# Fifteen small GpSimd operations of each setup of an S4D kernel, done by VectorE

## The chip, the cores and the metric

The kernel runs on one core of a Trainium2 chip. The metric is the device time of one execution in microseconds; a time is given as the median of several runs. The core has five engines, each with its own queue of instructions that it works off in order: TensorE (PE in the profile, its weight loads PEld), VectorE (DVE), ScalarE (ACT), GpSimd (POOL) and SyncE (SP), which here issues almost all DMA transfers.

## The reference

Four layers follow each other on an input x of 2048 tokens by 512 features, all in float32: an S4D convolution, a routed feed-forward layer, and both once more with the same weights. Each adds its result to x. Cut to what matters:

```
def A(u):                                   # S4D convolution, per feature d
    dt = exp(log_dt)
    A  = -exp(log_A_real) + 1j * A_imag     # 512 x 128
    C  = (C_real + 1j * C_imag) * dt[:, None]
    P  = exp((A * dt[:, None])[:, :, None] * arange(2048))
    K  = 2 * einsum("dn,dnl->dl", C, P).real
    y  = irfft(rfft(u, 4096) * rfft(K, 4096))[:2048]
    return y + u * D_skip

def B(x):                                   # two tokens of 2048, SwiGLU, 512 -> 1792 -> 512
    ...

x = x + A(layernorm(x)); x = x + B(layernorm(x))
x = x + A(layernorm(x)); x = x + B(layernorm(x))
```

The change lies in the preparation of the kernel K: from C_real, C_imag, A_imag, log_A_real and dt, the phase and the magnitude of C and of the powers of exp(A dt) are worked out per state n and feature d.

## The kernel before, in words

The 512 features are worked in four chunks of 128. The first convolution has two halves that run side by side. The first makes K: states lie on the 128 partitions, and for each group of 16 features (class KStep, 32 steps) a phase table and a decay table are built from a few powers, turned into sine and cosine, multiplied, and contracted over the states on TensorE. The second is the convolution itself by a transform in stages, mostly matmuls.

Before the first KStep, `setup` (line 543) turns the parameters into the starting powers. It is called twice: for chunk 0 (tiles of 128 by 128, called small here, in one tile named su) with its results left in SBUF, and for chunks 1 to 3 together (128 by 384, called wide, in tiles named su_w, su_w3b and su_bigB), whose results go to DRAM (pid, prd) and are loaded back per half chunk (tiles near and far). Each call returns a list of single instructions: absolute values of C, the arc tangent of their ratio (L586 to L594), its sine and cosine for the magnitude of C (L596 to L600), the phase by quadrant (L602 to L612), and integer phases of the powers (L615 to L636) and their decays (L641).

What the first setup makes is needed at once: L636 gives the integers from which ScalarE's L500 starts the table "eight" of the first eight phases; GpSimd's L504 and L507 fill that and the table "far", L669 builds a step's phase table, L683 and L688 its decay table. VectorE's L710, L712 and L717 multiply these with ScalarE's sine and cosine (L699, L702) into the tile sc, which TensorE contracts at L725; ScalarE's L729 and VectorE's L732 take the result (kt), TensorE transforms it at L745, and ScalarE's L755 copies that. The tables of a step have two buffers each, sine and cosine one.

In between, the statistics of the input x are taken on VectorE (L1005, 16 instructions over four loads of 1 MB, L1002). The four loads use two buffers in turn, those that later hold the tiles xc and z. So the second load into either waits for the statistics of the first, and the loads of xc and z for the convolution (L441, issued one behind the other on SyncE's queue) wait for the last statistics. Tables made from the statistics (L1013 to L1024) and tile z are what ScalarE's L838 needs, the layer norm in front of the convolution.

The order of everything is written out by hand. `PLAN` gives each unit of work a number, by lane: `setup` and `setup2` are the lists of the two calls, `stat0` the statistics, `table` their tables, `phase8`, `decay8`, `phase`, `decay`, `trig`, `prod_b`, `prod_p` and `contract` the KSteps. All units are sorted by that number and issued in turn, and `in_order` (line 389) ties the instructions of each engine to that order, SyncE's too. An instruction that waits therefore holds everything behind it on its engine. In this order the first setup's units have the numbers 17 to 234, those of VectorE and of the changed operations 22 to 96, mixed with the first of the second setup, with statistics and loads; the second setup's go from 19 to 355. The unit of the first setup's L636 has number 91, that of the wide L598 159, that of the last statistics 161.

Of the kernel before, what the change touches and what calls it, by code (L numbers as in the profile page):

```python
# [14 lines left out]
OP = mybir.AluOpType  # L15
# [29 lines left out]
    w=[52],  # L45
# [357 lines left out]
def build(tc, x, xr, lar, aim, cr, ci, ldt, dsk, wr, wg, wu, wd, d1_h, d1k_h, d4_h, w2_h, w3_h, w3b_h, sm_h, out):  # L403
# [3 lines left out]
    V, A, G, T = nc.vector, nc.scalar, nc.gpsimd, nc.tensor  # L407
    AX = mybir.AxisListType.X
    ctx = ExitStack()
    with ctx, in_order(tc, ORDER):  # L410
# [132 lines left out]
        def setup(c0, c1, room, direct=False):  # L543
# [6 lines left out]
            crt, cit, im, lr, sw, mx = (at_(i) for i in range(6))  # L550
            pc, ip = pair(26), pair(28).bitcast(I32)
            ar, ai, w, at, al = (at_(i) for i in range(20, 25))
# [24 lines left out]
            S = []  # L577
# [9 lines left out]
            S.append(lambda: A.activation(ai, cit, AF.Abs))  # L587
            S.append(lambda: V.tensor_tensor(mx, ar, ai, op=OP.max))
            S.append(lambda: V.tensor_tensor(sw, ar, ai, op=OP.min))
            S.append(lambda: G.tensor_scalar(w, mx, 1e-37, None, op0=OP.max))  # L590
            S.append(lambda: V.reciprocal(w, w))
            S.append(lambda: G.tensor_tensor(w, sw, w, op=OP.mult))
            S.append(lambda: A.activation(at, w, AF.Arctan))
            S.append(lambda: V.tensor_tensor(w, ai, ar, op=OP.is_gt))  # L594
            S.append(lambda: A.activation(al, lr, AF.Exp))
            S.append(lambda: A.activation(ar, at, AF.Sin))  # L596
            S.append(lambda: A.activation(ai, at, AF.Sin, scale=-1.0, bias=halfpi))
            S.append(lambda: G.tensor_tensor(mx, mx, ai, op=OP.mult))  # L598
            S.append(lambda: G.tensor_tensor(sw, sw, ar, op=OP.mult))
            S.append(lambda: G.tensor_tensor(mx, mx, sw, op=OP.add))  # L600
            g1, v1 = ar, ai
            S.append(lambda: G.tensor_scalar(g1, at, 1.0 / (2 * math.pi), None, op0=OP.mult))  # L602
            S.append(lambda: G.tensor_scalar(v1, g1, -2.0, 0.25, op0=OP.mult, op1=OP.add))
            S.append(lambda: G.tensor_tensor(v1, v1, w, op=OP.mult))
            S.append(lambda: G.tensor_tensor(g1, g1, v1, op=OP.add))
            S.append(lambda: V.scalar_tensor_tensor(al, al, -1.0, dt, op0=OP.mult, op1=OP.mult))
            S.append(lambda: G.tensor_scalar(v1, g1, -2.0, 0.5, op0=OP.mult, op1=OP.add))
            S.append(lambda: G.tensor_scalar(w, crt, 0.0, None, op0=OP.is_lt))
            S.append(lambda: G.tensor_tensor(v1, v1, w, op=OP.mult))
            S.append(lambda: G.tensor_tensor(g1, g1, v1, op=OP.add))  # L610
            S.append(lambda: G.tensor_scalar(v1, cit, 0.0, -0.5, op0=OP.is_lt, op1=OP.add))
            S.append(lambda: G.tensor_tensor(g1, g1, v1, op=OP.mult))  # L612
            u, gi = im, sw.bitcast(I32)
            bq, bi = pair(8), pair(22).bitcast(I32)
            S.append(lambda: V.scalar_tensor_tensor(u, im, 1.0 / (2 * math.pi), dt, op0=OP.mult, op1=OP.mult))  # L615
# [412 lines left out]

        st1, rd1 = stats_tiles(1)
        late_setup = setup(1, 4, [sb.tile([128, 32, CH], F32, name=f"su1_{k}", tag=k, bufs=1) for k in ("w3", "w3b", "bigB")])  # L1030

        xw = []
# [146 lines left out]
        for f_ in setup(0, 1, [new_big("su0", "A")], True):  # L1179
            put_in("setup", f_)  # L1180
# [686 lines left out]
```

## Time and profile before

| | us |
|---|---|
| median of 3 runs | 535.35 |
| lowest and highest | 533.23, 535.77 |
| the profiled execution, its own time | 532.64 |
| span of the profiled execution | 530.9 |

| engine | busy us | share of the span | instructions |
|---|---|---|---|
| TensorE | 432.4 | 81% | 5428 |
| VectorE | 411.9 | 78% | 957 |
| ScalarE | 385.2 | 73% | 862 |
| GpSimd | 340.0 | 64% | 364 |

The page also draws the span in 40 slices of 13.3 us. TensorE is nearly idle in the first four and nearly full from the eighth on; GpSimd is nearly full from the second to the ninth. The shares are averages over stages with different limits, so the first 140 us are read by stretch, from the views below. A row of a timeline gives the start and the length in us, the engine, the line of the kernel, the operation, what it writes and reads with their shapes, and in brackets how long the engine had been idle before and what ended it. The profiled execution is one of several, so its rows are set against its own time.

### The profile page before, as it was taken

The numbers are of one execution on the slowest core, as the hardware profiler recorded it, in microseconds if no ns is written. First come the engines' busy times: TensorE is split into PE (matmuls) and PEld (weight loads), VectorE is DVE, ScalarE is ACT, GpSimd is POOL, SyncE is SP. The second block draws the span as 40 slices with busy tenths as digits, with TensorE's granted clock in tenths as the row PEclk, the third lists the DMA queues.
The fourth block names the chain that finished last, engine by engine and source line by source line (L and its number), as shares of the span: only waits on it lengthen the run. The fifth ranks groups of instructions, "written<-read, shape, count | busy, mean of one in ns | idle before, by whom it ended". The sixth has DMA issues, their size and how long they took to land. (4 is left out here: it accounts for less than half of the span.)

```text
span 530.9 us, 14080 instructions
## 1 busy us (share of the span) xinstructions
PE 432.4 (81%) x5428; PEld 338.9 (64%) x5428; DVE 411.9 (78%) x957; ACT 385.2 (73%) x862; POOL 340.0 (64%) x364
## 2 busy tenths in 40 slices
PE   1011467999999999999989985899799999998486
PEld 1011345889878987689847853676678888664234
DVE  7878779787888899888977479675567689799851
ACT  6578999999999997889635435451566965769882
POOL 3898999998886778683503942254606878888200
PEclk9999999999999999999999998899799999999779
DMA  6825456988669787967767799536664857752943
GB/s 199 329 86 219 141 199 194 332 224 213 154 171 246 178 201 235 275 174 219 206 193 235 303 343 422 206 120 199 214 224 160 255 140 228 211 200 120 406 188 161
DMA packets 67307, 115.77 MB, mean 218 GB/s; under 512 B 8708, under 2 KB 50984, under 8 KB 62504
## 3 DMA queue, kind: packets, MB, share of 16 engines
q1 hardware_dynamic: 67112, 114.85, 66.8%
q8 instruction: 43, 0.70, 0.6%
q14 instruction: 24, 0.20, 0.1%
q0 software_dynamic: 128, 0.02, 0.0%
HBM read 68.83 MB, written 39.72 MB: 204 GB/s over the span
## 5 line engine op out<-in xcount | busy, mean ns | idle before, releaser
L873 POOL TENSOR_TENSOR y<-p 64x256 f32<-64x256 f32 x76 | 57.6, 758 | 71.0 <-DVE p L858 38.8
L717 DVE TENSOR_TENSOR sc<-tr,mg 128x1024 f32<-128x1024 f32 x64 | 77.0, 1210 | 1.1 <-POOL mg L688 0.8
L725 PE MATMUL pk<-sc 128*32 128x64 f32 x2048 | 39.0, 233 | 46.3 <-DVE sc L717 30.8
L725 PEld LDWEIGHTS pk<-sc 128*32 128x32 f32 x2048 | 33.4, 118 | 58.3 <-ACT tr L699 31.7
L683 POOL TENSOR_TENSOR mg<-eight,far 128x768 f32<-128x768 f32 x32 | 53.6, 1674 | 17.7 <-DVE sc L712 10.0
L669 POOL TENSOR_TENSOR ph<-eight,far 128x768 int32<-128x768 int32 x32 | 53.2, 1665 | 8.7 <-ACT tr L702 8.3
L849 DVE STREAM_TRANSPOSE g<-zf 128x512 f32<-128x512 f32 x64 | 45.5, 712 | 12.9 <-PE zf L845 11.4
L845 PE MATMUL zf<-z,d 128*128 128x256 f32 x192 | 53.6, 411 | 2.2 <-ACT z L1630 1.1
L1102 ACT ACTIVATE w<-pv 128x512 f32<-128x512 f32 x48 | 28.5, 594 | 35.2 <-PE pv L879 19.1
L879 PE MATMUL pv<-y,w 128*128 128x128 f32 x320 | 47.0, 294 | 4.3 <-POOL y L871 4.3
L879 PEld LDWEIGHTS pv<-y,w 128*128 128x128 f32 x320 | 41.8, 201 | 12.3 <-POOL y L871 9.2
L858 DVE TENSOR_TENSOR p<-pu,kf 128x1024 f32<-128x1024 f32 x32 | 38.9, 1219 | 13.1 <-PE pu L768 4.8
L745 PE MATMUL kq<-d1k,kt 128*64 128x128 f32 x512 | 38.5, 297 | 12.6 <-DVE kt L732 11.2
L768 PE MATMUL pu<-g,w 128*64 128x128 f32 x640 | 43.0, 278 | 0.4 <-DVE p L858 0.4
L745 PEld LDWEIGHTS kq<-d1k,kt 128*64 128x64 f32 x512 | 30.2, 147 | 20.7 <-DVE kt L732 15.6
L845 PEld LDWEIGHTS zf<-z,d 128*128 128x128 f32 x192 | 34.6, 198 | 13.5 <-DVE g L849 4.4
L768 PEld LDWEIGHTS pu<-g,w 128*64 128x64 f32 x640 | 36.4, 134 | 7.3 <-issue 4.2
L871 POOL TENSOR_TENSOR y<-p 64x256 f32<-64x256 f32 x52 | 38.4, 739 | 3.0
L688 POOL TENSOR_TENSOR mg<-mg,f32s 128x512 f32<-128x512 f32 x32 | 34.4, 1078 | 8.6 <-ACT mg L677 7.5
L827 PE MATMUL pv<-p,w 128*128 128x128 f32 x192 | 38.7, 283 | 0.0
L827 PE MATMUL pv<-p,w3b 128*128 128x128 f32 x192 | 37.2, 276 | 0.0
L699 ACT ACTIVATE tr<-ph 128x1024 f32<-128x1024 int32 x32 | 32.9, 1028 | 4.7 <-DVE sc L717 3.0
(380 smaller groups left out, 1149.9 us busy)
## 6 DMA issues: line engine op xcount, KB each, us to landing
vd<-w SPq DMA_DIRECT2D x48, 256.0 KB, 2.8
v<-vd SPq DMA_DIRECT2D x24, 512.0 KB, 6.8
kf<-kfd SPq DMA_DIRECT2D x16, 512.0 KB, 4.8
wd<-in_wd SPq DMA_DIRECT2D x4, 2048.0 KB, 12.2
ks<-kd SPq DMA_DIRECT2D x48, 128.0 KB, 3.4
kfd<-kd SPq DMA_DIRECT2D x24, 256.0 KB, 3.8
x<-in_xr SPq DMA_DIRECT2D x4, 1024.0 KB, 6.8
w<-in_w SPq DMA_DIRECT2D x2, 2048.0 KB, 8.1
```

The costliest lines, as they stand in the source:

```text
L669: G.tensor_tensor(self.ph[:, :, 8:32].rearrange("p d (k i) -> p d k i", k=3), self.first(0).rearrange("p d (o i) -> p d o i", o=1).to_broa ...
L683: G.tensor_tensor(mg[:, :, 0:2, 8:32].rearrange("p d t (k i) -> p d t k i", k=3), self.first(1).rearrange("p (d t o) i -> p d t o i", t=2, ...
L717: V.tensor_tensor(sc.rearrange("p d (t i) -> p d t i", t=3)[:, :, 0:3:2, :], t, self.mg[:, :, 0:3:2, :], op=OP.mult)
L725: T.matmul(self.pk[32 * g : 32 * g + 32, e, :], t[:, 0:32], t[:, 32:96], start=k == 1, stop=k == 0, tile_position=(0, 32 * g))
L745: T.matmul(self.pq[64 * ri : 64 * ri + 64, e].rearrange("p k g -> p (k g)"), self.kt[:, e].rearrange("p h b -> p (h b)"), d1k[:, 128 * ri ...
L768: T.matmul(pt[64 * par : 64 * par + 64, ri, q, :], w2[:, k1, 64 * ri : 64 * ri + 64], col(src, k1), start=True, stop=True, tile_position=( ...
L827: T.matmul(pv[:, k, :], w[:, j, :], p[:, t, k % 2, k // 2, :], start=t == 0, stop=t == 1)
L845: T.matmul(pf[:, 16 * s : 16 * s + 16, :], d1[:, 128 * s : 128 * s + 128], z[:, :, 16 * q : 16 * q + 16], start=True, stop=True)
L849: V.transpose(g[:, :, 16 * q : 16 * q + 16, :].rearrange("p k e t -> p e k t"), pf.rearrange("p (k t) e -> p e k t", t=2))
L858: V.tensor_tensor(pp, pu.rearrange("p (o r) q e -> p o r (q e)", o=1).to_broadcast([128, 2, 2, 2 * CH]), kf.rearrange("p r (o q) e -> p r ...
L873: E.tensor_tensor(y[0:64, :, par, :], p[0][ls, 0], p[1][ls, 1], op=OP.subtract)
L879: T.matmul(pv[:, k, :], w3[:, 4 * gi + k, :], y[:, k // 2, k % 2, :], start=True, stop=True)
```

## The change

In `setup`, 15 operations are issued on VectorE (V) instead of GpSimd (G): L590, L592, L598 to L600, L602 to L605 and L607 to L612. Since `setup` is called twice this moves 15 small and 15 wide instructions. What they compute, their operands, their place in PLAN and all else stay as they are.

```diff
--- before.py
+++ after.py
@@ -587,29 +587,29 @@
             S.append(lambda: A.activation(ai, cit, AF.Abs))
             S.append(lambda: V.tensor_tensor(mx, ar, ai, op=OP.max))
             S.append(lambda: V.tensor_tensor(sw, ar, ai, op=OP.min))
-            S.append(lambda: G.tensor_scalar(w, mx, 1e-37, None, op0=OP.max))
+            S.append(lambda: V.tensor_scalar(w, mx, 1e-37, None, op0=OP.max))
             S.append(lambda: V.reciprocal(w, w))
-            S.append(lambda: G.tensor_tensor(w, sw, w, op=OP.mult))
+            S.append(lambda: V.tensor_tensor(w, sw, w, op=OP.mult))
             S.append(lambda: A.activation(at, w, AF.Arctan))
             S.append(lambda: V.tensor_tensor(w, ai, ar, op=OP.is_gt))
             S.append(lambda: A.activation(al, lr, AF.Exp))
             S.append(lambda: A.activation(ar, at, AF.Sin))
             S.append(lambda: A.activation(ai, at, AF.Sin, scale=-1.0, bias=halfpi))
-            S.append(lambda: G.tensor_tensor(mx, mx, ai, op=OP.mult))
-            S.append(lambda: G.tensor_tensor(sw, sw, ar, op=OP.mult))
-            S.append(lambda: G.tensor_tensor(mx, mx, sw, op=OP.add))
+            S.append(lambda: V.tensor_tensor(mx, mx, ai, op=OP.mult))
+            S.append(lambda: V.tensor_tensor(sw, sw, ar, op=OP.mult))
+            S.append(lambda: V.tensor_tensor(mx, mx, sw, op=OP.add))
             g1, v1 = ar, ai
-            S.append(lambda: G.tensor_scalar(g1, at, 1.0 / (2 * math.pi), None, op0=OP.mult))
-            S.append(lambda: G.tensor_scalar(v1, g1, -2.0, 0.25, op0=OP.mult, op1=OP.add))
-            S.append(lambda: G.tensor_tensor(v1, v1, w, op=OP.mult))
-            S.append(lambda: G.tensor_tensor(g1, g1, v1, op=OP.add))
+            S.append(lambda: V.tensor_scalar(g1, at, 1.0 / (2 * math.pi), None, op0=OP.mult))
+            S.append(lambda: V.tensor_scalar(v1, g1, -2.0, 0.25, op0=OP.mult, op1=OP.add))
+            S.append(lambda: V.tensor_tensor(v1, v1, w, op=OP.mult))
+            S.append(lambda: V.tensor_tensor(g1, g1, v1, op=OP.add))
             S.append(lambda: V.scalar_tensor_tensor(al, al, -1.0, dt, op0=OP.mult, op1=OP.mult))
-            S.append(lambda: G.tensor_scalar(v1, g1, -2.0, 0.5, op0=OP.mult, op1=OP.add))
-            S.append(lambda: G.tensor_scalar(w, crt, 0.0, None, op0=OP.is_lt))
-            S.append(lambda: G.tensor_tensor(v1, v1, w, op=OP.mult))
-            S.append(lambda: G.tensor_tensor(g1, g1, v1, op=OP.add))
-            S.append(lambda: G.tensor_scalar(v1, cit, 0.0, -0.5, op0=OP.is_lt, op1=OP.add))
-            S.append(lambda: G.tensor_tensor(g1, g1, v1, op=OP.mult))
+            S.append(lambda: V.tensor_scalar(v1, g1, -2.0, 0.5, op0=OP.mult, op1=OP.add))
+            S.append(lambda: V.tensor_scalar(w, crt, 0.0, None, op0=OP.is_lt))
+            S.append(lambda: V.tensor_tensor(v1, v1, w, op=OP.mult))
+            S.append(lambda: V.tensor_tensor(g1, g1, v1, op=OP.add))
+            S.append(lambda: V.tensor_scalar(v1, cit, 0.0, -0.5, op0=OP.is_lt, op1=OP.add))
+            S.append(lambda: V.tensor_tensor(g1, g1, v1, op=OP.mult))
             u, gi = im, sw.bitcast(I32)
             bq, bi = pair(8), pair(22).bitcast(I32)
             S.append(lambda: V.scalar_tensor_tensor(u, im, 1.0 / (2 * math.pi), dt, op0=OP.mult, op1=OP.mult))
```

## Rows read from the trace of the kernel before

**Rows 1.** Busy time of each engine in four stretches (us from the start of the span; the length; then busy us and instructions of TensorE, its weight loads, VectorE, ScalarE and GpSimd; the granted clock, the busy share of the DMA engines, GB/s).

```profile
21.40:37.26 15.86, 0.00 (x0) 0.00 (x0) 10.87 (x18) 13.01 (x20) 15.38 (x14) 1.00 0.47 174
51.80:77.00 25.20, 11.72 (x240) 9.80 (x240) 18.81 (x22) 24.73 (x47) 24.64 (x23) 1.00 0.52 180
77.00:97.00 20.00, 16.45 (x345) 12.18 (x346) 17.64 (x27) 19.40 (x32) 19.22 (x19) 1.00 0.72 235
97.00:140.00 43.00, 42.62 (x702) 39.34 (x701) 34.58 (x51) 41.47 (x76) 38.92 (x36) 1.00 0.82 227
```

**Rows 2.** The waits of ScalarE from 51 to 97 us: who waited for whom, us in total, times, the longest.

```profile
ACT z L838 <- DVE su_w3b L628: 1.3, 1, 1.3
ACT gk L755 <- PE kq L745: 0.4, 1, 0.4
ACT mg L677 <- POOL eight L504: 0.3, 1, 0.3
```

**Rows 3.** The load of tile z: the last statistics on VectorE, the issue of the load on SyncE's queue, the time to landing in the view of the tile, and the first instruction on ScalarE that reads it (start us, us, engine, line, operation).

```profile
42.25 0.68 DVE L1005 BATCH_NORM_STATS2 stt<-x 128x6 f32<-128x512 f32 x1
...
43.38 0.38 SPq L441 DMA_DIRECT2D z<-in_x  x1
...
DMA to landing us min/median/max: 8.3/8.3/8.3
...
51.79 0.49 ACT L838 ACTIVATE z<-z,bz,rs 128x128 f32<-128x128 f32 x1 [1.27 <-DVE su_w3b L628]
```

**Rows 4.** GpSimd's operations of the setups: busy time and count on the small tile of the first setup from 5 to 20 us, and on the wide tile of the second from 5 to 70 us (all of its operations but L600).

```profile
5.00:20.00 15.00, 7.34 (x15) 1.00 0.83 285
...
5.00:70.00 65.00, 15.56 (x14) 1.00 0.57 205
```

**Rows 5.** VectorE from 7.6 to 21.5 us in order of time (start us, us, operation; in brackets the idle time before it and what ended it).

```profile
7.63 0.67 DVE L588 TENSOR_TENSOR su_w<-su_bigB 128x384 f32<-128x384 f32 x1 [0.28 <-ACT su_bigB L586]
...
8.42 0.88 DVE L615 SCALAR_TENSOR_TENSOR su_w<-su_w,dtb 128x384 f32<-128x384 f32 x1
...
9.95 0.28 DVE L594 TENSOR_TENSOR su<-su 128x128 f32<-128x128 f32 x1
10.15 0.55 DVE L589 TENSOR_TENSOR su_w<-su_bigB 128x384 f32<-128x384 f32 x1
10.62 0.42 DVE L619 TENSOR_TENSOR su<-su 128x256 f32<-128x256 f32 x1
11.07 0.29 DVE L620 TENSOR_SCALAR su<-su 128x256 int32<-128x256 f32 x1
11.28 0.35 DVE L616 TENSOR_SCALAR su_bigB<-su_w 128x384 f32<-128x384 f32 x1
11.55 0.61 DVE L622 TENSOR_SCALAR su_w<-su_w 128x384 f32<-128x384 f32 x1
12.08 0.68 DVE L628 TENSOR_SCALAR far<-su 128x256 int32<-128x256 int32 x2
12.68 0.53 DVE L628 TENSOR_SCALAR su<-su 128x256 int32<-128x256 int32 x1
...
14.16 0.56 DVE L628 TENSOR_SCALAR su<-su 128x256 int32<-128x256 int32 x1
...
18.58 0.96 DVE L625 TENSOR_SCALAR su<-su 128x256 int32<-128x256 f32 x1
19.89 0.23 DVE L634 TENSOR_SCALAR su<-su 128x128 int32<-128x128 f32 x1 [0.34 <-POOL su L600]
20.15 0.29 DVE L635 CUSTOM_DVE_ANT_0 su<-su 128x256 uint16<-128x256 uint16 x1
20.36 0.28 DVE L628 TENSOR_SCALAR su<-su 128x256 int32<-128x256 int32 x1
20.57 0.28 DVE L636 TENSOR_SCALAR su<-su 128x256 int32<-128x256 int32 x1
...
20.97 0.55 DVE L606 SCALAR_TENSOR_TENSOR su_bigB<-su_bigB,dtb 128x384 f32<-128x384 f32 x1
```

**Rows 6.** ScalarE's first sine, its first copy of the first setup's integers, and what that releases on GpSimd.

```profile
11.01 0.31 ACT L596 ACTIVATE su<-su 128x128 f32<-128x128 f32 x1
...
20.89 0.44 ACT L500 ACTIVATE eight<-su 128x256 int16<-128x256 int16 x1 [3.60 <-DVE su L636]
...
21.40 3.58 POOL L504 TENSOR_TENSOR eight<-eight,su 128x128 int32<-128x128 int32 x5 [1.54 <-ACT eight L500]
```

**Rows 7.** VectorE's statistics after the first load that it waits for, GpSimd's second L688, and VectorE's third L717.

```profile
24.69 1.88 DVE L1005 BATCH_NORM_STATS2 stt<-x 128x6 f32<-128x512 f32 x3 [1.97 <-DMA x<-in_xr]
...
36.20 1.06 POOL L688 TENSOR_TENSOR mg<-mg,f32s 128x512 f32<-128x512 f32 x1
...
38.94 1.21 DVE L717 TENSOR_TENSOR sc<-tr,mg 128x1024 f32<-128x1024 f32 x1
```

**Rows 8.** Two wide VectorE operations of one shape in the second setup.

```profile
44.72 0.99 DVE L619 TENSOR_TENSOR su_bigB<-su_bigB 128x768 f32<-128x768 f32 x1
...
64.19 1.79 DVE L624 TENSOR_TENSOR su_w<-su_w,su_bigB 128x768 f32<-128x768 f32 x1
```

**Rows 9.** The waits of ScalarE for L699 from 8 to 52 us.

```profile
ACT tr L699 <- DVE sc L717: 2.6, 1, 2.6
ACT tr L699 <- POOL ph L669: 0.9, 1, 0.9
```

## The prediction

> **What bounds the kernel now.** I read first the table of busy time by stretch [rows 1]. From 97 to 140 us TensorE is busy for 42.6 of 43 us, so whatever comes late or early in the first 97 us is passed on whole by TensorE's fixed order, and nothing of the change lies behind that point. Before 97 us TensorE is half idle and ScalarE and GpSimd are the full engines: from 51.8 to 77 they are busy for 24.73 and 24.64 of 25.2 us. The reader is to see that two engines, not one, are full there. Emptying GpSimd can shorten that stretch only by what ScalarE waits for it. The waits of ScalarE [rows 2] name that: 0.3 us, in one place, beside 0.4 us for TensorE. So I then asked what starts ScalarE's full stretch. It is L838 at 51.79, the first use of tile z; z's load was issued at 43.38 and landed 8.3 us later, at 51.7 [rows 3]. The list of waits puts that stop down to VectorE's L628, but the landing is what fits the time. The load in turn is issued behind the load of xc on SyncE's queue, and xc's buffer is free only after the last statistics, L1005 on VectorE at 42.25 [rows 3]. So the path is: VectorE up to 42.9 us, load of z, ScalarE to about 97 us, TensorE to the end.
>
> **The change, part by part.** GpSimd loses the 15 small operations of the first setup, 7.34 us by the one row that groups them, and the 15 wide ones of the second, of which the row of their tile groups 14 with 15.56 us [rows 4]. On GpSimd this is worth next to nothing by rows 2.
>
> *The first setup on VectorE, to L636.* L636 at 20.57 releases L500 on ScalarE at 20.89, which had waited 3.60 us, and that releases GpSimd's L504 at 21.40 [rows 5, 6]. All 15 small operations now stand ahead of L636 in VectorE's order, and the wide L590 and L592 with them.
> - The first two small ones cost nothing: VectorE waits 0.28 us for ScalarE until 7.63 behind them, and they go in ahead of that without the hand-overs between the two engines [rows 5].
> - The other 13: a small tensor_tensor costs 0.20 from start to start when the next does not need it (L594 at 9.95, L589 at 10.15), and its 0.28 plus 0.03 when it does (L619 takes 0.42 and L620 starts 0.45 after it). A small tensor_scalar costs 0.26 then (L634 to L635) [rows 5]. Half of them feed the next one, so 13 x 0.25 = 3.2 us; 2.6 if none waits, 4.0 if all do.
> - The wide ones: 0.47 for L592 (as the wide L589, 10.15 to 10.62) and 0.3 for L590 (as L616 wide, 11.28 to 11.55) [rows 5]: 0.8 us.
> - A new wait: L599 needs ScalarE's L596, which ends at 11.32 [rows 6]. VectorE gets there at about 10.5 (L619's start at 10.62, 0.3 later for L590, 0.3 to 0.4 earlier for wide L615), because L619 and L620, which ran meanwhile, now stand behind it. 0.8 us, with everything of VectorE queued behind.
> - One wait goes: L634 waited 0.34 for GpSimd's L600 [rows 5].
> - VectorE's other operations get cheaper. Those that ran beside GpSimd's took longer than their twins that did not: wide L615 0.88 against wide L606 0.55; L628 at 12.68 and 14.16 0.53 and 0.56 against 0.28 at 20.36; L625 0.96 against L620's 0.29; wide L622 0.53 from start to start against L616's 0.27; the two L628 at 12.08 0.60 against 0.42 [rows 5]. Given back: 0.33 + 0.25 + 0.28 + 0.67 + 0.26 + 0.18 = 2.0 us.
>
> Sum: 3.2 + 0.8 + 0.8 - 0.3 - 2.0 = 2.5 us later at L636. The bounds are 1.9 (no small operation waits for the one before) and 4.5 (nothing given back). I take 2.5, since each slow row lies beside a GpSimd row and each quick one does not.
>
> The Trainium skill speaks to this on the page SBUF — State Buffer, section Who interferes with whom: a VectorE instruction with two SBUF inputs, or in a two-port mode, and a GpSimd instruction exclude each other, and the second waits until the first is through. The trace agrees in kind (0.88 against 0.55); by the rule the whole 2.0 us comes back, without it none and the sum is 4.5.
>
> *From L636 to the load of z.* VectorE itself has 1.97 us of waiting for a load ahead of L1005 at 24.69 [rows 7]: 0.5 of the 2.5 is left. GpSimd is busy for 15.38 of 15.86 us from 21.40 to 37.26, the end of the second L688 (36.20 + 1.06) [rows 1, 7], so this L688 ends at 39.8, and VectorE's L717, which ran at 38.94, must wait for it: 0.8 us late. The larger counts. Then the wide L598 stands ahead of the last L1005: 0.5 us (0.47 as L589). The load of z goes out 1.3 us late and L838 starts at about 53.1. ScalarE gets there in time: its line, late by about 1.8 through the same L688 and L669, ends 1.27 us ahead of 51.79 today [rows 3]. L599 wide must wait for ScalarE's L596 on VectorE, but the tables that L838 also needs are then ready near 51.6 to 52.5, under the same cover; with the load not late they would decide.
>
> *The second setup, 51.8 to 77 us.* Eight wide operations go into VectorE's order, 0.3 to 0.5 us each by the wide rows [rows 5], some 2.4 to 4.4 us with their waits for each other. VectorE is busy for 18.81 of 25.2 us there [rows 1], so 6.4 us of idle time hide them. GpSimd runs ahead, and the 0.3 us of rows 2 go.
>
> Sum: +1.3 - 0.3 = +1.0 us on the profiled execution's 532.64 (span 530.9). That execution is 2.7 us below the median shown, 535.35. On the median the forecast is 536.3. Its own range: from -0.5 (lower bound, and all of ScalarE's 1.1 us idle time from 51.8 to 97 gone) to +3.4 (L636 late by 4.5, so 2.8 at L717, L598 at 0.88, less 0.3), 534.9 to 538.8.
>
> **The rivals.**
> - *VectorE becomes the bound of 51.8 to 77 us: slower.* GpSimd is still busy there, with L669, L683, L688 and L504, for some 15.7 us (24.64 less eight at 15.56 / 14), and a moved operation with two SBUF inputs may wait for one of them. The price is that of L624, 1.79 us, against 0.99 for L619 of the same shape [rows 8]: 0.8 us more each. Eight operations at 0.5 + 0.8 are 10.4 us, over 6.4 idle, so 4.0 late, with the 1.3 of the load 5.3: 540.6. It decides from a mean of 0.8 us each (6.4 / 8), and is plain to measure from 1.0. For it: VectorE's gaps are few and lie before given instructions. Against: GpSimd is only 60% busy once the moved work is gone, and VectorE's own wide operations gain by that. The Trainium skill has the rule, on SBUF — State Buffer, section Who interferes with whom: the one that starts second blocks fully.
> - *GpSimd was the bound: faster.* If ScalarE's order only follows GpSimd's pace, and the first setup, with no hand-over between two engines, is done sooner, ScalarE's waits go: 2.6 and 0.9 us for L699, 1.3 for L838, 0.3 for L677 [rows 2, 9]. That is 5.1 us: 530.2. For it: GpSimd's full stretch. Against: 2.6 of it hangs on a VectorE instruction and 1.3 on z's load, and neither is GpSimd's.
> - *All of it hidden.* If L636 is late by under 1.9, both waits behind it take it up, and L598's 0.5 less 0.3 is left: 535.5.
>
> **How the numbers follow.** About 0.5%, 2.7 us, can be told from no change. Forecast 0.42 (0.38 of it within that bound, 0.04 slower), VectorE as the bound 0.28 (0.26 slower, 0.02 within), all hidden 0.18 (within), GpSimd as the bound 0.12 (0.10 faster, 0.02 within). So faster 0.10, same 0.60, slower 0.30. The time is that of the likeliest, 536.3. The range takes the forecast's own, nearly all of the hidden case, and the lower two thirds of VectorE's: 533.4 to 540.0.
>
> **What would show it.** In the changed kernel: L636 at 22.5 to 23.5 instead of 20.57; a wait of VectorE for ScalarE's L596 near 10.5; wide L615 near 0.55; GpSimd's L504 at about 23.9; the load of z issued at about 44.7 and L838 at 53.1; ScalarE busy for over 24 of the 25 us behind it, GpSimd for some 15; TensorE full from about 98. The prediction is wrong if L838 keeps its time, if ScalarE's stretch shows gaps that end on VectorE, or if the stretch from L838 to TensorE's full part gets shorter by more than 1 us.

## The result and the profile after

| | before | after |
|---|---|---|
| median of 18 runs, us | 534.85 | 539.95 |
| lowest and highest | 531.95, 538.17 | 535.62, 542.86 |
| the profiled execution, its span | 532.64, 530.9 | 535.62, 533.8 |
| VectorE, GpSimd busy us | 411.9, 340.0 | 422.3, 316.5 |

The ratio is 1.0076, with a 95% interval of 1.0053 to 1.0099: 4.1 us slower (2.8 to 5.3), where 1.0 was forecast; the two medians lie 5.1 us apart. A later comparison of the same two kernels gave 1.0071 (1.0033 to 1.0109). The loss is made before 97 us. As its mark I use VectorE's only L1026, which stands in a fixed place of its order: it starts at 92.71 us before and at 97.34 after, 4.63 later.

```profile
92.71 0.66 DVE L1026 TENSOR_REDUCE swr<-wrt 128x1 f32<-128x512 f32 x1
```

```profile
97.34 0.67 DVE L1026 TENSOR_REDUCE swr<-wrt 128x1 f32<-128x512 f32 x1
```

VectorE in the first setup, after (start us, us, operation, idle time and what ended it), to be read against [rows 5]:

```profile
8.51 0.56 DVE L615 SCALAR_TENSOR_TENSOR su_w<-su_w,dtb 128x384 f32<-128x384 f32 x1
...
11.33 0.29 DVE L599 TENSOR_TENSOR su<-su 128x128 f32<-128x128 f32 x1 [0.72 <-ACT su L596]
...
14.77 0.28 DVE L628 TENSOR_SCALAR su<-su 128x256 int32<-128x256 int32 x1
...
23.25 0.29 DVE L636 TENSOR_SCALAR su<-su 128x256 int32<-128x256 int32 x1
```

The first setup came out as forecast. L636 starts at 23.25 instead of 20.57. VectorE now waits 0.72 us for ScalarE's L596, and wide L615 (0.56) and L628 (0.28) are quick now that GpSimd is silent beside them.

VectorE from there to the load of z, after; [rows 3, 7] answer to it:

```profile
33.73 1.28 DVE L1005 BATCH_NORM_STATS2 stt<-x 128x6 f32<-128x512 f32 x2 [1.56 <-DMA x<-in_xr]
34.93 0.67 DVE L710 SCALAR_TENSOR_TENSOR sc<-tr,mg 128x512 f32<-128x512 f32 x1
...
40.16 1.21 DVE L717 TENSOR_TENSOR sc<-tr,mg 128x1024 f32<-128x1024 f32 x1
...
43.76 0.68 DVE L1005 BATCH_NORM_STATS2 stt<-x 128x6 f32<-128x512 f32 x1
```

Of the 2.7 us, 1.2 are left at L710 (33.70 before). What VectorE waits for ahead of it is a load of x, not GpSimd. The same wait stands there before:

```profile
32.50 1.29 DVE L1005 BATCH_NORM_STATS2 stt<-x 128x6 f32<-128x512 f32 x2 [3.01 <-DMA x<-in_xr]
```

GpSimd's second L688 ends at 39.8 (38.77 + 1.06) as forecast, but VectorE reaches its L717 only at 40.16, straight behind its own work. With L598 and the rest the last statistics start 1.51 us late.

The load of z and the first instruction that uses it, after:

```profile
44.89 0.38 SPq L441 DMA_DIRECT2D z<-in_x  x1
...
DMA to landing us min/median/max: 6.8/6.8/6.8
...
54.90 1.65 ACT L838 ACTIVATE z<-z,bz,rs 128x128 f32<-128x128 f32 x4 [2.51 <-DVE bz L1024]
```

This load takes 6.8 us instead of 8.3: it lands at 51.7 as before, and its late issue costs nothing. With 8.3 us it would have landed at 53.2. L838 starts at 54.90, 3.11 us late, and stops for VectorE's L1024, the end of the tables, through at 54.87. Before, L1024 was through at 50.3, 1.4 us ahead of z. VectorE from the first of the tables to their last, after, and then the same stretch before:

```profile
44.58 0.18 DVE L1015 TENSOR_TENSOR rs<-stt 128x16 f32<-128x16 f32 x1
45.63 0.56 DVE L599 TENSOR_TENSOR su_w<-su_w,su_bigB 128x384 f32<-128x384 f32 x1 [0.87 <-ACT su_bigB L596]
...
46.40 0.90 DVE L600 TENSOR_TENSOR su_w<-su_w 128x384 f32<-128x384 f32 x1
47.22 1.98 DVE L618 CAST su_bigB<-su_bigB 128x768 int32<-128x768 f32 x1
...
49.24 1.69 DVE L619 TENSOR_TENSOR su_bigB<-su_bigB 128x768 f32<-128x768 f32 x1
...
51.98 1.30 DVE L628 TENSOR_SCALAR su_w3b<-su_bigB 128x768 int32<-128x768 int32 x1
...
54.69 0.18 DVE L1024 SCALAR_TENSOR_TENSOR bz<-mv,rs 128x16 f32<-128x16 f32 x1
```

```profile
43.07 0.18 DVE L1015 TENSOR_TENSOR rs<-stt 128x16 f32<-128x16 f32 x1
...
43.49 0.55 DVE L618 CAST su_bigB<-su_bigB 128x768 int32<-128x768 f32 x1
...
47.07 0.70 DVE L628 TENSOR_SCALAR su_w3b<-su_bigB 128x768 int32<-128x768 int32 x1
...
50.15 0.17 DVE L1024 SCALAR_TENSOR_TENSOR bz<-mv,rs 128x16 f32<-128x16 f32 x1
```

GpSimd meanwhile, after:

```profile
46.37 0.52 POOL L504 TENSOR_TENSOR eight<-eight,su 128x128 int32<-128x128 int32 x1 [3.34 <-ACT eight L500]
46.84 1.95 POOL L683 TENSOR_TENSOR mg<-eight,far 128x768 f32<-128x768 f32 x1
48.75 1.37 POOL L688 TENSOR_TENSOR mg<-mg,f32s 128x512 f32<-128x512 f32 x1
50.08 2.78 POOL L504 TENSOR_TENSOR eight<-eight,su 128x256 int32<-128x256 int32 x2
```

From the start of L1015 to that of L1024 VectorE took 7.08 us before and takes 10.11 now, 3.0 more. Counted from the start of each operation to the start of the next, the wait for ScalarE, L599 and L600 are new, 2.2. L618 goes from 0.55 to 1.98 us, but VectorE was idle for 0.60 behind it before and is not now, so that costs 0.75. L619 grows by 0.7 (0.99 in [rows 8], now 1.69), L628 by 0.6 (0.70, now 1.30). L620 and the small ones behind L710 are 1.3 quicker. L600, L618, L619 and L628, the slow ones, each begin while GpSimd's L504, L683 or L688 runs.

ScalarE's waits from 51 to 100 us, after, against [rows 2]:

```profile
ACT z L838 <- DVE bz L1024: 2.5, 1, 2.5
ACT su_w L641 <- DMA prd<-su_w: 1.4, 1, 1.4
```

The second wait, 1.4 us until 71.37, is a new one. L641 writes into a buffer whose store to DRAM (prd) must be read out first, and on SyncE's queue this store follows a store of pid. Queue, after:

```profile
66.06 0.32 SPq L575 DMA_DIRECT2D pid<-su_w3b  x1
66.42 0.43 SPq L575 DMA_DIRECT2D prd<-su_w  x1
```

Before, the two went out at 60.32 and 60.68. The store of pid waits for VectorE's wide L628, now at 65.48 behind L604 (1.72 us) and another L628 (1.99). Windows of after, to be set beside [rows 1]:

```profile
54.90:80.00 25.10, 10.64 (x232) 9.12 (x234) 22.98 (x33) 23.53 (x43) 11.62 (x10) 1.00 0.53 181
100.00:140.00 40.00, 39.56 (x680) 36.45 (x683) 32.37 (x46) 38.30 (x69) 36.10 (x30) 1.00 0.86 241
```

And GpSimd's waits from 52 to 90 us, after:

```profile
POOL mg L688 <- ACT mg L677: 11.7, 2, 11.3
```

From L838 on GpSimd is busy for 11.62 of 25.1 us and then stops 11.3 us for ScalarE. Its relief buys nothing.

### The profile page after: what moved, and what is told of

Same layout as the page of the kernel before. It is cut to its first block, busy times and chain, and to the rows that moved or that the text cites. A ratio compares the mean times of both kernels' runs of the same rounds, so it can differ in the third digit from the quotient of the medians.

```text
span 533.8 us, 14078 instructions
## 1 busy us (share of the span) xinstructions
PE 432.4 (81%) x5428; PEld 339.1 (64%) x5428; DVE 422.3 (79%) x987; ACT 385.5 (72%) x862; POOL 316.5 (59%) x334
## 5 line engine op out<-in xcount | busy, mean ns | idle before, releaser
L717 DVE TENSOR_TENSOR sc<-tr,mg 128x1024 f32<-128x1024 f32 x64 | 77.0, 1209 | 0.3
L683 POOL TENSOR_TENSOR mg<-eight,far 128x768 f32<-128x768 f32 x32 | 53.6, 1675 | 17.6 <-DVE sc L712 10.1
L669 POOL TENSOR_TENSOR ph<-eight,far 128x768 int32<-128x768 int32 x32 | 53.0, 1662 | 8.6 <-ACT tr L702 8.2
L845 PE MATMUL zf<-z,d 128*128 128x256 f32 x192 | 53.2, 409 | 2.2 <-ACT z L1630 1.1
L688 POOL TENSOR_TENSOR mg<-mg,f32s 128x512 f32<-128x512 f32 x32 | 34.4, 1077 | 20.6 <-ACT mg L677 19.6
L702 ACT ACTIVATE tr<-ph,cst 128x1024 f32<-128x1024 f32 x32 | 35.7, 1115 | 0.4
```

The source lines that it names most:

```text
L669: G.tensor_tensor(self.ph[:, :, 8:32].rearrange("p d (k i) -> p d k i", k=3), self.first(0).rearrange("p d (o i) -> p d o i", o=1).to_broa ...
L683: G.tensor_tensor(mg[:, :, 0:2, 8:32].rearrange("p d t (k i) -> p d t k i", k=3), self.first(1).rearrange("p (d t o) i -> p d t o i", t=2, ...
L717: V.tensor_tensor(sc.rearrange("p d (t i) -> p d t i", t=3)[:, :, 0:3:2, :], t, self.mg[:, :, 0:3:2, :], op=OP.mult)
L845: T.matmul(pf[:, 16 * s : 16 * s + 16, :], d1[:, 128 * s : 128 * s + 128], z[:, :, 16 * q : 16 * q + 16], start=True, stop=True)
```

## The experiments

Theory A: two places make the loss, the tables of the layer norm and the store of prd. The rival of the prediction was VectorE's sum of work; another, that the late L636 is enough. The mark L1026, from the one profiled execution of each kernel, stands beside every ratio (against the kernel before; its interval behind it).

| kernel | ratio (95%) | L838 | L1026 |
|---|---|---|---|
| before | 1 | 51.79 | 92.71 |
| after | 1.0076 (1.0053 to 1.0099) | 54.90 | 97.34 |
| after_again | 1.0071 (1.0033 to 1.0109) | 55.1 | 97.7 |
| small_only | 0.9992 (0.9963 to 1.0021) | 54.36 | 95.20 |
| wide_only | 1.0036 (0.9995 to 1.0076) | 53.97 | 96.20 |
| both_orders | 1.0018 (0.9989 to 1.0046) | 53.76 | 94.67 |
| tables_first | 1.0017 (0.998 to 1.0055) | 53.7 | 96.2 |
| store_first | 1.0007 (0.9976 to 1.0037) | 55.1 | 96.7 |
| late_wide_back | 1.0031 (0.9997 to 1.0065) | 56.43 | 97.57 |
| loads_first | 0.9913 (0.9877 to 0.995) | 49.78 | 91.6 |
| loads_again | 0.9964 (0.993 to 0.9999) | 49.6 | 91.7 |
| loads_orders | 0.9997 (0.9966 to 1.0029) | 53.7 | 95.3 |
| wide_loads | 0.9986 (0.9954 to 1.0018) | 51.1 | 92.0 |
| late_wide_loads | 0.9979 (0.9944 to 1.0015) | 51.3 | 92.7 |

**Halves of the change.** The 15 lines with an engine H; small_only has this one, wide_only the opposite:

```diff
+            H = V if direct else G
-            S.append(lambda: G.tensor_scalar(w, mx, 1e-37, None, op0=OP.max))
+            S.append(lambda: H.tensor_scalar(w, mx, 1e-37, None, op0=OP.max))
...
```

small_only: 

> Only the first setup's 15 small operations are on VectorE, the second setup's 15 wide ones stay on GpSimd. Landmarks are L838 on ScalarE (51.79 before, 54.90 after) and L1026 on VectorE (92.71 before, 97.34 after). Theory A (two delays in a row: the first setup costs 1.2 us through the loads of x, the rest is made by the wide operations on VectorE): L636 at about 23 as after, L710 for the first time at 34.5 to 35 (33.70 before), L838 at 53.0 to 53.5, L1026 at 94 to 94.7, time +1.3 to +2.0 us over before. Theory B (the first setup makes the whole loss): L838 at 54.5 to 55, L1026 at 97, time +4. Theory C (the wide operations make it, the first setup is hidden): L838 at 51.8, L1026 at 92.7, time +0.

wide_only: 

> Only the second setup's 15 wide operations are on VectorE, the first setup's 15 small ones stay on GpSimd. Theory A: L636 at 20.5 to 21.2, L838 at 52.5 to 53.5 because the tables of the statistics end late behind the wide L599 and L600, a wait of ScalarE of 1 to 1.5 us for the store of prd near 70, L1026 at 95 to 96, time +2.5 to +3.5 us over before. Theory B: L838 at 51.8 to 52.3, L1026 at 92.5 to 93.2, time +0 to +0.5. Theory C: L838 at 54.5 or more, L1026 at 97, time +4.

small_only, VectorE, and then the first use of z on ScalarE:

```profile
27.55 1.98 DVE L594 TENSOR_TENSOR su_bigB<-su_bigB 128x384 f32<-128x384 f32 x1
...
35.01 1.29 DVE L1005 BATCH_NORM_STATS2 stt<-x 128x6 f32<-128x512 f32 x2 [3.10 <-DMA x<-in_xr]
36.21 0.67 DVE L710 SCALAR_TENSOR_TENSOR sc<-tr,mg 128x512 f32<-128x512 f32 x1
```

```profile
54.36 1.65 ACT L838 ACTIVATE z<-z,bz,rs 128x128 f32<-128x128 f32 x4 [1.34 <-DVE su_w3b L628]
```

The small half is no cheaper at the front than the whole: wide L594 begins just behind the start of a L669 on GpSimd (27.48) and takes 1.98 us (0.62 before, near the end of one), the statistics behind it free a buffer of x late, the load into it is waited for 3.10 us, and L710 is 2.5 us late. Here it is z's load that decides, issued at 45.89 and landing 8.4 us later, at 54.3, as the prediction had it. The 1.2 us expected were too low, because a load of x hangs on the statistics ahead of it. wide_only has both places without the late L636 (19.98): L618 again takes 1.98, ScalarE is idle for 2.52 us ahead of L838 until L1024, and for 1.2 us for the store of prd. So VectorE's late L636 is not what makes them. At L1026 the two halves are 2.5 and 3.5 us late, more than the whole change together: they do not add up.

**The two orders.** Numbers in PLAN, on the kernel after; both_orders has both pairs, tables_first the first (wide L599 and L600 behind the tables), store_first the second (the store of prd ahead of that store of pid):

```diff
-        19, 30, 26, 32, 44, 41, 80, 81, 101, 117, 82, 165, 141, 159, 166, 172, 197, 199, 214, 216, 98, 232, 228, 247, 261, 268,
+        19, 30, 26, 32, 44, 41, 80, 81, 101, 117, 82, 165, 141, 159, 189.2, 189.4, 197, 199, 214, 216, 98, 232, 228, 247, 261, 268,
-        278, 288, 298, 341, 191, 209, 219, 99, 218, 259, 208, 109, 231, 246, 256, 270, 260, 262, 318, 250, 252, 355,
+        278, 288, 298, 341, 191, 209, 219, 99, 218, 231.5, 208, 109, 231, 246, 256, 270, 260, 262, 318, 250, 252, 355,
```

both_orders: 

> The changed kernel with two units moved in the written order and nothing else: the wide L599 and L600 behind the last table of the statistics (166 and 172 to 189.2 and 189.4), and the store of the second decay plane ahead of that of the fifth integer plane (259 to 231.5). Theory A (tables held up on VectorE, then ScalarE waiting for that store behind another store on SyncE's queue): L838 at 53.0 to 53.4, set by z's load, no wait of ScalarE for prd near 71, L1026 at 94 to 94.7, time +1.3 to +2 us over before. Rival (VectorE is too full from 54 to 80 us in any order, 23.75 of 26 us busy after): the two waits come back in other places, L1026 at 96.5 to 97.3, time +3.5 to +4.5.

tables_first: 

> The changed kernel with two numbers of PLAN alone altered: the wide L599 and L600 behind the layer norm's tables. Theory A (the tables were held up behind these two and behind the GpSimd work that they let meet the table instructions): L838 starts at 53.2 to 53.8 as with both edits, ScalarE still stops for 1.0 to 1.4 us before the wide L641 because the store of prd stays where it was, L1026 at 95.7 to 96.2, and a ratio near 1.004. Rival (the store is what counts, the tables are covered by something later): L1026 stays at 97 or later and the ratio at 1.007.

store_first: 

> The changed kernel with one number of PLAN alone altered: the second store of prd ahead of the store of pid that VectorE delays. Theory A: L838 stays at 54.5 to 55.0, the stop of ScalarE before the wide L641 goes (under 0.3 us), L1026 at 95.8 to 96.3, and a ratio near 1.004. Rival (the tables alone count and ScalarE would have stopped for something else in the same place): another wait of 1 us or more within 10 us of it, and L1026 at 97.

both_orders, VectorE in the same stretch:

```profile
44.88 0.55 DVE L618 CAST su_bigB<-su_bigB 128x768 int32<-128x768 f32 x1
...
47.73 1.87 DVE L620 TENSOR_SCALAR su_bigB<-su_bigB 128x768 int32<-128x768 f32 x1
...
51.64 1.05 DVE L955 TENSOR_TENSOR rq0b<-rq0b,rq0a 128x16 f32<-128x16 f32 x1
...
53.55 0.17 DVE L1024 SCALAR_TENSOR_TENSOR bz<-mv,rs 128x16 f32<-128x16 f32 x1
```

L618 now runs while GpSimd waits and takes 0.55 us; L620 and L955 are hit in its place (1.87 and 1.05), and L1024 comes 1.1 us earlier than in after. It still ends the wait of L838 (53.76, not the 53.0 to 53.4 expected): z's load, which was to set it, landed at 53.05. L1026 comes as expected with both (94.67) and with the tables alone (96.2); with the store alone it is later, 96.7. In tables_first ScalarE's stop for prd stays, 1.5 us; in store_first it is gone and the stop before L838 stays, 2.5 us. In store_first three short waits of ScalarE for TensorE, 0.8 us together, that after does not have, take half of the gain back: the rival's mechanism, though each is shorter than the 1 us that it named, and two come later. So the two places are separate; they are worth 1.1 and 0.6 us at L1026 alone and 2.7 together. By the clock the interval with both (up to 1.0046) lies below that of after (from 1.0053), though not below that of after_again (from 1.0033). The ratios of these three can't be told apart, nor from the kernel before. The 2.0 us that L1026 is still late with both are there at L838.

**The ten late wide ones back on GpSimd** (L602 to L605 and L607 to L612 of the second setup, on the kernel after):

```diff
-            S.append(lambda: V.tensor_scalar(g1, at, 1.0 / (2 * math.pi), None, op0=OP.mult))
+            S.append(lambda: H.tensor_scalar(g1, at, 1.0 / (2 * math.pi), None, op0=OP.mult))
...
```

late_wide_back: 

> The changed kernel with the wide L602 to L612 back on GpSimd; the small ones and the wide L590, L592 and L598 to L600 stay on VectorE. Theory A: L838 at 54.7 to 55 as after, since these ten stand behind it, no wait of ScalarE for the store of prd near 71, L1026 at 95.5 to 96, time +2.8 to +3.3 us over before. Rival 1 (these ten cost nothing): L1026 at 97.3, time +4. Rival 2 (GpSimd was a bound of this stretch after all and gets its work back): gaps of ScalarE that end on GpSimd, L1026 at 97 to 99.

The stop for prd went, as expected, and L838 came another 1.5 us later, as no theory had it: GpSimd's L504, L604 and L605 now lie beside the small operations of the tables. VectorE:

```profile
53.30 1.05 DVE L955 TENSOR_TENSOR rq0b<-rq0b,rq0a 128x16 f32<-128x16 f32 x1
54.38 0.91 DVE L957 TENSOR_SCALAR rq0b<-rq0b 128x16 f32<-128x16 f32 x1
55.33 0.17 DVE L959 TENSOR_TENSOR rs<-rq0a,rq0b 128x16 f32<-128x16 f32 x1
55.54 0.85 DVE L1024 SCALAR_TENSOR_TENSOR bz<-mv,rs 128x16 f32<-128x16 f32 x1
```

They take 0.17 us each in after, here up to 1.05. What was saved in one place was lost in the other: L1026 starts at 97.57 for 97.34.

**The loads of x.** VectorE's waits for them, 1.97 and 3.0 us before, stand ahead of the tables and of z's load. On the kernel before, the second load moves ahead of the weights on SyncE's queue, and the weights go behind all four:

```diff
-    x0=[105, 39, 125, 118],
-    w=[52],
+    x0=[39.5, 39, 125, 118],
+    w=[126.5],
```

loads_first: 

> The kernel before with the second load of x moved up on SyncE's queue, ahead of the weights, and those behind the other loads. If the load of x_0 is what VectorE waits for at 24.69 (1.97 us) and what it waits for there is passed on to z's load, then L710 starts at 31.8 to 32.5 instead of 33.70, the load of z goes out at 41.6 to 42.4, L838 starts near 50.1 to 50.8, L1026 near 91 to 91.8, and the kernel is faster by about 0.3%. Rival (the tables or GpSimd's L688 take the place of the load): L838 stays within 0.5 us of 51.79 and the time does not move.

loads_again: 

> The kernel before with the loads of x ahead of the weights, a second time, since its ratio (0.9913) is more than the 1.1 us by which its L1026 came earlier (91.6 against 92.71) account for. If the gain of 4 us and more belongs to the order, the ratio comes out at 0.990 to 0.994 again; if it was in part the scatter of single executions, which is some 3 us to either side, at 0.996 to 0.998.

loads_orders (this on both_orders): 

> The changed kernel with its three orders altered: tables ahead of the wide L599 and L600, the store of prd up, the loads of x ahead of the weights. If the three act one by one: L636 at 23.3, VectorE's waits of 1.6 and 1.6 us for the x loads get shorter, the load of z goes out 0.5 to 1.5 us earlier than with two of them (44.77), L838 at 52.5 to 53.5, L1026 at 93.5 to 94.5, and the time equal to that of the kernel before within 0.3%. Rival (once the loads are early, the phases that start 2.7 us late with L636 bind): the load of z at 44.5 or later and nothing gained over the two orders alone (1.0018).

In loads_first L710 starts at 32.1, L838 at 49.8, behind ScalarE's own work with no stop, L1026 at 91.6. It is faster than the kernel before in both comparisons, though the second interval ends at 0.9999, and no other kernel here is. The first ratio, 0.9913, is more than 1.1 us at L1026 account for; the second, 0.9964, is the case of scatter, so its worth lies nearer to 0.2 to 0.4% than to 0.9. On both_orders it gave nothing: L710 at 34.8, L838 at 53.7, L1026 at 95.3. The rival held there. The third and fourth load go out when the statistics of the first two free their buffers, and these stand behind the late setup in VectorE's order: they go out at 25.4 and 28.7 us with the second load early and without (22.7 and 26.0 in loads_first).

**Is GpSimd's relief worth something once the front is early?** loads_first has 1.7 and 1.2 us of ScalarE's waits that end on GpSimd. wide_loads is wide_only with all three orders; late_wide_loads moves only the ten late wide ones, with the store and the loads:

```diff
+            H = G if direct else V
...
-            S.append(lambda: G.tensor_scalar(g1, at, 1.0 / (2 * math.pi), None, op0=OP.mult))
+            S.append(lambda: H.tensor_scalar(g1, at, 1.0 / (2 * math.pi), None, op0=OP.mult))
...
```

wide_loads: 

> The wide operations alone on VectorE (the small ones stay on GpSimd), with all three orders altered. If what the change costs is the late L636 and the two held-up places, and GpSimd's relief is worth something once these are gone: L636 at 20 to 20.6, L838 at 49.8 to 50.8, ScalarE's waits for GpSimd of 1.7 (L699) and 1.2 us (L677), which the kernel with the early loads shows, under 1.5 together, L1026 at 90 to 91.6, and a ratio no worse than that of loads_again. Rival (VectorE, fuller by the wide work, is late by itself): L1026 at 92 or later and a ratio above loads_again by 0.3% or more.

late_wide_loads: 

> Of the change only the wide L602 to L605 and L607 to L612 on VectorE, whose place is behind the tables; the rest on GpSimd; the store of prd and the loads of x moved up. With the tables as in loads_again, L838 at 49.6 to 50.2; no GpSimd work of the setup beside VectorE's small table operations; ScalarE's wait for L504 (1.2 us) gone; L1026 at 90.5 to 91.6, and a ratio at or just below that of loads_again. Rival (the ten in VectorE's order hold up its own L628 and L710 behind them as in the changed kernel): a wait of ScalarE or TensorE for VectorE of over 0.5 us between 52 and 90 us and L1026 at 92 or later.

The wait of 1.2 us (L677 for L504) went in both; that of 1.7 us (L699) stayed, and a new one of 1.4 and 1.6 us ahead of L838, for L1024, came in. So L838 is at 51.1 and 51.3, not near 50 as expected, and neither kernel is measurably faster than the early loads alone. late_wide_loads beside loads_first shows why. In loads_first, VectorE's last table operations, and GpSimd:

```profile
48.45 0.17 DVE L955 TENSOR_TENSOR rq0b<-rq0b,rq0a 128x16 f32<-128x16 f32 x1
48.65 0.36 DVE L957 TENSOR_SCALAR rq0b<-rq0b 128x16 f32<-128x16 f32 x1
49.05 0.18 DVE L959 TENSOR_TENSOR rs<-rq0a,rq0b 128x16 f32<-128x16 f32 x1
49.26 0.17 DVE L1024 SCALAR_TENSOR_TENSOR bz<-mv,rs 128x16 f32<-128x16 f32 x1
```

```profile
48.46 1.20 POOL L602 TENSOR_SCALAR su_bigB<-su_bigB 128x384 f32<-128x384 f32 x1
49.75 0.69 POOL L603 TENSOR_SCALAR su_bigB<-su_bigB 128x384 f32<-128x384 f32 x1
```

The same in late_wide_loads:

```profile
48.45 0.98 DVE L955 TENSOR_TENSOR rq0b<-rq0b,rq0a 128x16 f32<-128x16 f32 x1
49.47 0.61 DVE L957 TENSOR_SCALAR rq0b<-rq0b 128x16 f32<-128x16 f32 x1
50.11 0.17 DVE L959 TENSOR_TENSOR rs<-rq0a,rq0b 128x16 f32<-128x16 f32 x1
50.32 0.97 DVE L1024 SCALAR_TENSOR_TENSOR bz<-mv,rs 128x16 f32<-128x16 f32 x1
```

```profile
48.35 1.05 POOL L688 TENSOR_TENSOR mg<-mg,f32s 128x512 f32<-128x512 f32 x1
49.37 1.89 POOL L504 TENSOR_TENSOR eight<-eight,su 128x256 int32<-128x256 int32 x2
```

Up to 48.4 us the two are alike. Where GpSimd had L602 and L603 of the setup, it now goes straight on to L688 and L504, and the four small VectorE operations beside them take 2.84 us from the first start to the last end instead of 0.98. L838 is 1.5 us later than in loads_first.

**The change a second time.** after_again is the changed kernel itself.

> The changed kernel itself a second time, against the kernel before on another chip or at another hour, because the kernels with a part of the change have ratios that lie 1 to 3 us under what their L1026 would give (small_only: 2.5 us later, 0.9992; late_wide_back: 4.9 us later, 1.0031). If the lateness at L1026 reaches the end whole, the ratio is 1.007 to 1.010 again. If some 2 us of it are taken up behind 140 us in most executions, 1.003 to 1.006.

1.0071: the first case. For the whole change the two ratios give 4.1 and 3.8 us, and the lateness at L1026 (4.6 and 5.0 us) lies within their intervals, so all of it may reach the end. Single profiled executions show this less plainly. The spans are 2.9 us longer for after and 4.3 for after_again, and from L1026 to the end the fourteen profiled executions take between 436.1 and 439.7 us. Why small_only, tables_first, store_first, late_wide_back and loads_orders lose some 3 us less by the clock than at L1026 is not settled. Single executions scatter by some 3 us to either side, and the intervals, 1.6 to 2.0 us to either side, explain only part of it.

## Why the prediction was right or wrong

- *What bounds the kernel.* Right. GpSimd freed for half of its time moved nothing, and what was late at L1026 in the whole change came out at the end as far as the intervals can tell (4.6 and 5.0 us there, 4.1 and 3.8 by the clock).
- *The first setup, +2.5 at L636.* Right, 2.68, with its terms: the new wait 0.72 for 0.8, all that was to be given back by quicker twins, the wait for L600 gone. The rule of the Trainium skill, SBUF — State Buffer, section Who interferes with whom, by which the whole of it comes back, agrees with this: 0.56 against 0.88 for wide L615.
- *Slack, L688, L598: +1.3 at z's load.* The size was right, 1.5, for a wrong reason. L688 was hidden. Behind the load of x that the prediction took as slack at 24.69 there is another, for which VectorE waited 3.01 us until 32.50. That one is issued only when the statistics ahead of it free its buffer, so late statistics make it late: it went out at 28.71 for 27.73.
- *z's load decides L838.* Wrong for the change. The load got quicker by what it was late, which no term of the sum had; but with the 8.3 us of before it would have landed at 53.2, still ahead of the tables. Right in small_only.
- *The tables "ready near 51.6 to 52.5, under the same cover".* This is the step that failed: 54.87. The prediction put in the wait, but not that L599 and L600 stand ahead of L618 in VectorE's order and that L618 and L619 behind them then meet GpSimd's L683 and L688, before which they had run. From L1015 to L1024 that made 3.0 us where the prediction left room for 0.9 at most. The cover was thin besides: before, the 1.4 us between tables and z were the wait for one late part of z's load, told of in the last section.
- *The second setup, hidden in 6.4 us of idle time.* Half right. VectorE had room (22.98 of 25.1 us busy), and yet the store that waits for one of its operations went out 5.7 us late (66.06 for 60.32), 2.6 more than L838, and through SyncE's queue that cost ScalarE 1.4 us. The prediction counted a sum where an order decides. The rival of VectorE priced the contention rightly (L604 1.72, L628 1.99), but as a sum over idle time, and that sum did fit in.
- *The sum.* +1.0 forecast, +4.1 measured. At L1026 it is 4.6: 3.1 at L838, from the tables, and 1.5 behind it, nearly all of it the stop for the store.
- *The range.* That the median, 539.95, lies inside it is luck. The forecast's own range ended at 538.8; the range reaches to 540.0 only by the rival of VectorE, and what that rival described, VectorE's work outgrowing its idle time, did not happen. By the 0.5% that the prediction calls the least to be told from no change, 0.76% is slower, and to that it gave 0.30.

## What to carry to other kernels

Work moved to an engine with idle time delays what stands behind it in that engine's order, and idle time in sum was no cover here: look up for each moved operation what follows it and who waits for that, on a DMA queue too. An engine that is relieved runs ahead into its next work, and that work falls beside other instructions than before; between VectorE and GpSimd this alone made four small operations 1.9 us longer in late_wide_loads. And a wait for a load is slack only if the load does not itself hang on the engine that waits.

## What the runs showed of the hardware

VectorE's small operations, 128 by 16, which took 0.17 us undisturbed, took 0.61 to 1.05 us when they began while GpSimd's two-input L504, L604, L605 or L688 ran, in late_wide_back and late_wide_loads. Each of these six ended 0.03 us after GpSimd's instruction (L955 at 54.35, L504 at 54.32): what they cost is what was left of GpSimd's. L959, which began 0.01 us ahead of one in either run, kept its 0.17. Beside GpSimd's L602, of one input, the same four took 0.17 to 0.36 in loads_first, and it was L602 that was long, 1.20 us against 0.69 for L603 of the same shape. The Trainium skill (SBUF — State Buffer, section Who interferes with whom) says that whoever is first holds the shared ports for its whole instruction; the rows with L504 agree, those with L602 do not show it.

The load of z took 6.8 to 8.4 us to land (issued at 44.8 it took 6.8 us in late_wide_back and 8.3 in both_orders; loads_first and loads_again, one kernel, have 8.1 and 6.9): a change of 1.5 us in a load's issue can vanish in that. The traces record 16 landings for it. Outside wide_loads, which has two late ones, fifteen are in 6.7 to 6.9 us after the issue, and the sixteenth comes within 0.5 us of them or, in before, small_only, both_orders, loads_first and loads_orders, 1.4 to 1.5 us behind. In these five, a packet of 16 KB on the DMA queue that the profile calls instruction began 0.8 to 1.5 us ahead of the fifteenth landing, in the other eight 0.3 to 0.6 us. That this packet held up the last part is likely but not shown, since the traces do not name the DMA engine of a packet.
